# A decode attention kernel: one critical section with recorded semaphores, and a TensorE loop over six of the eight head groups

## The chip, the cores and the metric

The kernel runs on one core of one Trainium2 chip. The time is the device time of that core in microseconds (us), and the median of several runs is quoted. The span in the profile, from the first instruction to the last, is about 2 us shorter than the time.

## The reference

A decode step with adaptive layer norm: attention over a long cache, then a gated MLP mixer. The sizes are four sequences (B = 4), one new token each, 32 heads, 4096 cached positions, head size 128, width 512, all bf16. Cut to what matters:

```python
q = (h @ wq).reshape(B, Sq, H, Dh).transpose(0, 2, 1, 3)
scores = einsum('bhqd,bhkd->bhqk', q, k_cache) * Dh ** -0.5
p = softmax(scores)
o = einsum('bhqk,bhkd->bhqd', p, v_cache)
x = x + ga * (o.transpose(0, 2, 1, 3).reshape(B, Sq, H * Dh) @ wo)
h = layernorm(x) * (1 + cb) + sb
x = x + gb * gmlp(h, w_in, w_sp, b_sp, w_out)
```

The K and V caches are 268 MB of the 283 MB that the kernel reads.

## The kernel before

The work is cut into 32 quads: 8 groups of 4 heads, times 4 sequences. A quad loads 4 MiB of K and 4 MiB of V, each as 128 rows of 32 KB, one row per partition. VectorE multiplies K by q in two halves, TensorE sums over the head size with identity matmuls, VectorE folds and does the softmax, and TensorE multiplies by V one quad later.

```python
def load(cache, i, tag, parts):
    t = kvp.tile([P, NT * DH], BF16, name=tag, bufs=2)
    ...
        nc.sync.dma_start(out=t[:, a:b], in_=kv_view(cache, i)[:, a:b])
...
def scores(i, half):
    ...
    nc.vector.tensor_tensor(out=kt, in0=kt, in1=q[:, None, :].to_broadcast([P, HT, DH]), op=ALU.mult)
    ps = psum.tile([P, HT, DC], F32, name="s_ps", bufs=2)
    for cc in range(DH // DC):                       # 16 matmuls of 128x512
        nc.tensor.matmul(ps, lhsT=ident, rhs=kt[:, :, cc * DC:(cc + 1) * DC],
                         start=(cc == 0), stop=(cc == DH // DC - 1))
...
for i in range(NQ):                                  # 32 quads, written out
    if i + 1 < NQ:
        st["k", i + 1] = load_k(i + 1)
    if quads[i][1] == 0: ...                         # wo of this group, two buffers
    st["v", i] = load_v(i)
    if i == NQ - 1: ...                              # last wo, then w_in and w_out
    if i > 1:
        diagonal(i - 2)
    scores(i, 0)
    if i > 1:
        project(i - 2)
    scores(i, 1)
    fold(i, 0); fold(i, 1); softmax(i)               # order differs in the last quads
    if i > 0:
        values(i - 1)                                # 32 matmuls on V
    if i > 1:
        apply(i - 2)                                 # with wo, once per group
```

All tiles come from pools, a framework places the semaphores, and TensorE's whole instruction stream is straight-line.

## Time and profile before

| | before |
|---|---|
| time, median of three runs | 667.66 us (667.34 to 667.72) |
| span in the profile | 665.5 us |
| bytes read | 282.73 MB |
| rate in steady state | 432 GB/s, DMA share 1.00 |
| TensorE, VectorE busy | 62%, 61% |

The page of the kernel before. Its first line is the busy time of each engine (us, share of the span, instructions). The queue lines give packets, MB and the share of 16 DMA engines' span. Then comes the chain of work that ended last, by engine. Two lines of the costliest groups follow: the score matmuls and the fold, with busy time, mean ns of one, the engine's idle time before them and what ended it. The last line is the group of K loads: count, KB each, median us from issue to landing.

```profile
PE 415.7 (62%) x3024; PEld 204.6 (31%) x3024; DVE 402.6 (61%) x475; ACT 41.3 (6%) x115; POOL 4.7 (1%) x21
...
q1 hardware_dynamic: 12640, 282.73, 98.9%
q8 instruction: 23, 0.38, 0.2%
...
DMA 62%; PE 24%; DVE 12%; issue 0%; SPq 0%; ACT 0%; DVEq 0%
...
L281 PE MATMUL s_ps<-kt,ident 128*128 128x512 bf16 x1024 | 293.5, 457 | 185.5 <-DVE kt L276 185.5
...
L290 DVE TENSOR_REDUCE S<-s_ps 128x64 f32<-128x512 f32 x64 | 44.3, 692 | 125.5 <-PE s_ps L281 125.5
...
kt<-in_A_k_cache_dram SPq DMA_DIRECT2D x31, 4096.0 KB, 26.0
```

The hardware queue fills the engines (98.9% of their span). The second queue line counts the instruction fetches: 23 packets, 0.38 MB, so 16 KB each.

The stretches view of the same kernel: window, its length, then busy time and instruction count of PE, PEld, DVE, ACT and POOL, then the granted TensorE clock, the DMA share and GB/s.

```profile
60.00:300.00 240.00, 154.38 (x1036) 74.53 (x1035) 151.08 (x168) 12.59 (x39) 0.00 (x0) 0.77 1.00 432
300.00:600.00 300.00, 185.20 (x1209) 89.08 (x1209) 189.27 (x202) 14.46 (x45) 0.00 (x0) 0.76 1.00 432
```

In steady state the DMA engines do not rest (share 1.00).

The timeline of the sync engine, which issues nearly all loads (start us, us the issuing instruction took, engine, line, what):

```profile
0.75 0.37 SPq L74 DMA_DIRECT2D vt<-in_w_mod_dram  x1
...
643.21 0.37 SPq L444 DMA_DIRECT2D win_434<-in_B_w_in_dram  x1
648.07 1.44 SPq L444 DMA_DIRECT2D win_435<-in_B_w_in_dram  x1
650.51 0.34 SPq L446 DMA_DIRECT2D wout_436<-in_B_w_out_dram  x1
651.74 0.33 SPq L446 DMA_DIRECT2D wout_437<-in_B_w_out_dram  x1
663.16 0.36 SPq L545 DMA_DIRECT2D out_dram<-ot  x1
```

The first load is issued at 0.75 us, the output at 663.16 us, 2.3 us before the end of the span.

### The profile page before, as it was taken

To read this page: it belongs to the slowest core of one execution; us is meant where nothing else is said; L and a number is where in the kernel's file an instruction comes from. 1 tells how busy PE (TensorE), PEld (TensorE's weight loads), DVE (VectorE), ACT (ScalarE), POOL (GpSimd) and SP (SyncE) were. 2 spreads that over 40 slices of the span, in tenths; PEclk is the share of its full clock that TensorE was granted. 3 is DMA by queue.
4 is the path that set the end of the run, shared out by engine and by line. 5 is a ranking of instruction groups with operands and counts; after the bars stand their busy time and mean duration, and the time that the engine had idled before them with its cause. 6 is when DMAs were issued, how large, how long until landed. Compare 5 with 4: busy or idle time off the path is not lost.

```text
span 665.5 us, 6939 instructions
## 1 busy us (share of the span) xinstructions
PE 415.7 (62%) x3024; PEld 204.6 (31%) x3024; DVE 402.6 (61%) x475; ACT 41.3 (6%) x115; POOL 4.7 (1%) x21
## 2 busy tenths in 40 slices
PE   2557776655677655676555477654657655657775
PEld 2223333222333322233222233232223322223334
DVE  2166776675556576547666456666555666655762
ACT  1200000000000000000000000000000000000002
POOL 2000000000000000000000000000000000000000
PEclk9977777668887667887667788676888766888795
DMA  9999999999999999999999999999999999999995
GB/s 379 439 425 427 437 439 424 429 438 434 427 428 441 428 428 434 435 426 434 433 436 424 436 435 430 423 439 435 428 431 435 433 430 432 437 426 435 428 417 236
DMA packets 12749, 283.17 MB, mean 426 GB/s; under 512 B 1448, under 2 KB 1968, under 8 KB 4016
## 3 DMA queue, kind: packets, MB, share of 16 engines
q1 hardware_dynamic: 12640, 282.73, 98.9%
q8 instruction: 23, 0.38, 0.2%
q14 instruction: 6, 0.05, 0.0%
q0 software_dynamic: 64, 0.00, 0.0%
q10 hardware_dynamic: 16, 0.01, 0.0%
HBM read 282.73 MB, written 0.00 MB: 425 GB/s over the span
## 4 chain that ended last, share of the span: by engine, by line
DMA 62%; PE 24%; DVE 12%; issue 0%; SPq 0%; ACT 0%; DVEq 0%
DMA kt<-in_A_k_cache_dram 58%; PE s_ps L281 24%; DVE kt L276 11%; DMA vt<-in_A_v_cache_dram 3%; DMA wout_437<-in_B_w_out_dram 1%; PE big L341 0%; DVE S L290 0%; ACT E L311 0%; SPq L92 0%; DVE P_1_109 L314 0%; DVE P_0_105 L314 0%; PE y_ps L522 0%; DVE nm L308 0%; DVE mT L300 0%; SPq L78 0%
## 5 line engine op out<-in xcount | busy, mean ns | idle before, releaser
L281 PE MATMUL s_ps<-kt,ident 128*128 128x512 bf16 x1024 | 293.5, 457 | 185.5 <-DVE kt L276 185.5
L276 DVE TENSOR_TENSOR kt<-kt,qbc 128x8192 bf16<-128x8192 bf16 x64 | 282.7, 4420 | 82.9 <-DMA kt<-in_A_k_cache_dram 82.9
L281 PEld LDWEIGHTS <-ident 128*128 128x128 bf16 x1024 | 116.4, 114 | 351.1 <-issue 229.8
L290 DVE TENSOR_REDUCE S<-s_ps 128x64 f32<-128x512 f32 x64 | 44.3, 692 | 125.5 <-PE s_ps L281 125.5
L354 PE MATMUL zo_ps<-sel,osb 128*128 128x4 f32 x248 | 33.2, 257 | 26.6 <-ACT osb L347 26.6
L311 ACT ACTIVATE E<-S,nm 128x128 f32<-128x128 f32 x32 | 12.8, 401 | 563.4 <-DVE nm L308 563.4
L354 PEld LDWEIGHTS zo_ps<-sel,osb 128*128 128x128 f32 x248 | 30.6, 194 | 38.4 <-ACT osb L347 38.4
L341 PE MATMUL big<-vt,P_0_105 128*32 128x512 bf16 x352 | 21.0, 380 | 1.5 <-DMA vt<-in_A_v_cache_dram 1.5
L341 PE MATMUL big<-vt,P_1_109 128*32 128x512 bf16 x320 | 19.1, 380 | 0.0
L341 PE MATMUL big<-vt,P_2_113 128*32 128x512 bf16 x320 | 19.1, 380 | 0.0
L347 ACT COPY osb<-big 128x512 f32<-128x512 f32 x31 | 17.6, 566 | 20.0 <-PE big L341 20.0
L215 PE MATMUL big<-vt,hbc 128*32 128x512 bf16 x128 | 9.6, 471 | 5.2 <-DMA vt<-in_A_wq_dram 5.2
L314 DVE TENSOR_TENSOR P_1_109<-E,mask_99 128x512 bf16<-128x512 f32 x11 | 7.6, 692 | 6.8 <-ACT E L311 6.8
L314 DVE TENSOR_TENSOR P_0_105<-E,mask_99 128x512 bf16<-128x512 f32 x11 | 7.6, 692 | 6.7 <-ACT E L311 6.7
L341 PEld LDWEIGHTS <-P_0_105 128*32 128x32 bf16 x352 | 8.4, 96 | 8.9 <-DMA vt<-in_A_v_cache_dram 1.6
L314 DVE TENSOR_TENSOR P_2_113<-E,mask_99 128x512 bf16<-128x512 f32 x10 | 6.9, 692 | 6.2 <-ACT E L311 6.2
L400 PE MATMUL attn_ps<-oP,wo_g 128*128 128x4 bf16 x112 | 3.8, 164 | 10.6 <-DVE oP L397 10.6
L341 PEld LDWEIGHTS <-P_1_109 128*32 128x32 bf16 x320 | 7.6, 96 | 6.7
L341 PEld LDWEIGHTS <-P_2_113 128*32 128x32 bf16 x320 | 7.6, 96 | 6.7
L375 DVE TENSOR_TENSOR oT<-zo_ps,rz 128x4 bf16<-128x4 f32 x32 | 5.4, 168 | 7.1 <-PE zo_ps L363 6.0
L215 PEld LDWEIGHTS <-hbc 128*32 128x32 bf16 x128 | 4.4, 114 | 10.3 <-issue 8.4
L308 DVE STREAM_TRANSPOSE nm<-hb 128x32 f32<-128x32 f32 x32 | 6.8, 212 | 1.1
(221 smaller groups left out, 131.1 us busy)
## 6 DMA issues: line engine op xcount, KB each, us to landing
kt<-in_A_k_cache_dram SPq DMA_DIRECT2D x31, 4096.0 KB, 26.0
vt<-in_A_v_cache_dram SPq DMA_DIRECT2D x31, 4096.0 KB, 33.7
vt<-in_A_wq_dram SPq DMA_DIRECT2D x1, 4096.0 KB, 20.4
kt<-in_A_k_cache_dram SPq DMA_DIRECT2D x2, 2048.0 KB, 24.8
wo_g<-in_A_wo_dram SPq DMA_DIRECT2D x7, 512.0 KB, 26.5
vt<-in_w_mod_dram SPq DMA_DIRECT2D x1, 3072.0 KB, 9.8
vt<-in_A_v_cache_dram SPq DMA_DIRECT2D x1, 2048.0 KB, 17.8
win_434<-in_B_w_in_dram SPq DMA_DIRECT2D x1, 1344.0 KB
```

The lines of the kernel that those rows point to most:

```text
L215: nc.tensor.matmul(qp[hl * R:(hl + 1) * R, 0:n], lhsT=hbc[:, j, b, :], rhs=wv[:, g0:g0 + n, hl, :], start=(j == 0), stop=(j == J - 1), til ...
L276: nc.vector.tensor_tensor(out=kt, in0=kt, in1=q[:, None, :].to_broadcast([P, HT, DH]), op=ALU.mult,)
L281: nc.tensor.matmul(ps, lhsT=ident, rhs=kt[:, :, cc * DC:(cc + 1) * DC], start=(cc == 0), stop=(cc == DH // DC - 1),)
L290: nc.vector.tensor_reduce(out=st["S", i][:, half * HT:(half + 1) * HT], in_=st.pop(("s", i, half)), axis=AX.X, op=ALU.add,)
L308: nc.vector.transpose(out=nm, in_=hb)
L311: nc.scalar.activation(out=E, in_=S, func=AF.Exp, bias=nm[:, 0:1], scale=att_scale, accum_out=rs,)
L314: nc.vector.tensor_tensor(out=P4[:, 0:NT, :], in0=E[:, :, None].to_broadcast([P, NT, NH]), in1=mask4[:, None, :].to_broadcast([P, NT, NH]) ...
L341: nc.tensor.matmul(po[32 * t:32 * t + 32], lhsT=P4[:, n0:n0 + 8, :], rhs=st["v", i][:, n0:n0 + 4, :], start=(u == 0), stop=(u == NU - 1), ...
L347: nc.scalar.copy(out=osb, in_=po)
L354: nc.tensor.matmul(st["o", i], lhsT=osb[:, n, :], rhs=sel[:, NH * n:NH * n + NH], start=(n == 0), stop=(n == 3),)
L375: nc.vector.tensor_tensor(out=oT[:, :, b], in0=st.pop(("o", i)), in1=rz, op=ALU.mult,)
L400: nc.tensor.matmul(attn_ps[:, jo, :], lhsT=(wo_g[:, hl] if g < G - 1 else wo_l[hl // 2][:, hl % 2])[:, jo * P:(jo + 1) * P], rhs=oT[:, hl, :],
```

## The change

The intent is to take scheduling, buffers and semaphores out of the framework's hands, and to make TensorE's program short. A recorder collects every operation, works out which earlier ones it must wait for, and emits everything in one critical section, with one semaphore for each engine and one for each DMA buffer ("lane"). TensorE's instructions of groups 1 to 6 become one loop body of four quads, run six times, with waits that grow with the pass number. Fixed buffers replace the rotating ones, wo has one buffer and is loaded one group later, there are four P buffers instead of three, and w_in and w_out get lanes of their own. The diff, cut to its core:

```diff
+class Recorder:
+    ...                      # record(): what each operation must wait for
+    def emit(self, periods):
+        ...
+                if e == "tensor" and lo <= k < hi:
+                    if k == lo:
+                        with engine.Fori(0, periods, 1) as it:
+                            for group in body:
+                                ...
+                                    engine.wait_ge(sm, it * d + v)
+                                issue(group[0])
+                    continue
+                for w in o.waits:
+                    engine.wait_ge(sem(w), w.value)
+                issue(o)
...
-    nc = tc.nc
-    ctx.enter_context(tc.manual_schedule())
+    nc = Recorder(tc.nc, tc)
...
-        t = kvp.tile([P, NT * DH], BF16, name=tag, bufs=2)
+    kts = [kvp.tile([P, NT * DH], BF16, name=f"kt{a}", align_bytes=128) for a in range(2)]
+    vts = [kvp.tile([P, NT * DH], BF16, name=f"vt{a}", align_bytes=128) for a in range(2)]
...
-    NB = 3
+    NB = 4
...
-                    st["wo", g] = wk.tile([P, NH, D], BF16, name="wo_g", bufs=2)
-                    nc.sync.dma_start(out=st["wo", g], in_=wo_w[g])
+            if b == 0 and first > 0:
+                nc.sync.dma_start(out=wo_g, in_=wo_w[g - 1], lane="wo")
...
-                    nc.sync.dma_start(out=win[a], in_=win_v[:, j0:j1, :])
+                    nc.sync.dma_start(out=win[a], in_=win_v[:, j0:j1, :], lane=f"win{a}")
...
+        load(A_k_cache, kts[0], 0, 0, (1,), "k0")
+        for i in range(B + 1):
+            step(i // B, i % B, i)
+        nc.mark()
+        for i in range(B + 1, NQ - B + 1):
+            step(i // B, i % B)
+        nc.mark()
...
+        with tc.tile_critical():
+            nc.emit(G - 2)
```

## The prediction

> **What bounds the kernel now.** The DMA stream. The queue table gives the hardware queue 282.73 MB and 98.9% of the 16 engines' span. The windows view, in 40 us stretches from 60 to 620 us, shows a DMA share of 1.00 and 431 to 433 GB/s in every one. [...] The bytes take 282.73 / 0.432 = 654 us of the 665.5 us span; the rest is start and tail.

> The chain of waits names K loads 58%, score matmuls 24%, the VectorE multiply 11%. Compute is not critical: a K load takes 26 us from issue to landing, but its own 4.19 MB need only 9.7 us. So some 16 us of work is queued ahead of each, and K buffers could come free many us later before the engines idle. TensorE and VectorE each work about 25 of 40 us (two quads): 7 us of slack per quad.

> **What the change does.**
> - Same matmuls, VectorE and ScalarE work and bytes. K and V keep two buffers; the wo loads move one group later (0.5 MB, 1.2 us of stream) but stay before the last V load: 0.
> - The loop adds five backward branches. [...] No trace here shows how long; even 5 us falls where TensorE idles 5 to 7 us anyway (timeline before the first score matmul of a quad), with 16 us of queued DMA behind: 0. Instruction fetch is 0.2% of DMA; [...].
> - One semaphore per buffer instead of eight shared: w_in and w_out are issued with the last V load instead of at 643 to 652 us (the sync queue's waits: 13.7 and 1.9 us on earlier transfers). The stream ends near 658 instead of 661 us. But the tail follows the last V piece (653.0) and wo piece (654.3), which land as before; the matmuls on w_in wait for h (657.7), those on the second w_out half wait about 0.2 us: -0.2.
> - Weight loads are no longer issued ahead of their matmul's wait: about 0.1 us (one weight load's duration) on some three handovers of the tail: +0.3.
> - Entry and exit of the critical section: [...].
> - Start: group 0's wo no longer pads the queue before K load 3 (issued at 45.1 us, the queue lasting to about 48): +0.1.

> Sum: +0.5 us, all critical.

> **Prediction.** 668.2 us, 8 in 10 between 665.8 and 670.5. Faster by over 2%: 1%; within 2%: 97%; slower by over 2%: 2%.

> **What would show it.** Right: DMA share 1.00 at 432 GB/s in every 40 us window, span within 2 us of 665.5; w_in and w_out issued near 631 us; TensorE idle at loop edges without a dip of DMA. Wrong on the loop: DMA share below 0.95 in slices 80 us apart. Wrong on the tail: clearly other than 12 us from the last V landing to the end.

> **What would make it wrong.** Instruction fetch taking over 15 us per loop edge; other SBUF addresses of K and V changing the DMA rate; early w_in loads overtaking the last V pieces.

The terms that are left come to +0.2 us (0, 0, −0.2, +0.3, +0.1). The sum of +0.5 us also holds the +0.3 us of the cut term, an estimate for which no measured number was named. The loop's 0: TensorE waits 185.5 us in 33 waits for VectorE's product on the page before, 5.6 us each in the mean.

## More of the kernel before

The two compute engines have idle time, but that alone does not say how much compute could be added: the engines take turns (on the page TensorE waits 185.5 us for VectorE's product, and VectorE 125.5 us for TensorE's sums). The chain of work that ended last, in order of time (start us, us, what), shows it at the start, where data for the first quads is already there:

```profile
31.29 4.43 DVE kt L276
35.77 9.28 PE s_ps L281 x32
45.07 0.70 DVE S L290
...
48.48 4.34 DVE kt L276
52.85 9.27 PE s_ps L281 x32
...
69.93 9.27 PE s_ps L281 x32
```

From one quad's score matmuls to the next is 17.08 us (52.85 − 35.77, and again 69.93 − 52.85). This is the serial compute cycle: multiply 4.4, matmuls 9.3, fold 0.7, softmax and a remainder of 2.7. Further on a quad takes about 19.7 us of stream, an estimate from its 8.52 MB (K, V and a quarter of wo) at the 432 GB/s above, so only some 2.6 us per quad are to spare.

## The result, and the profile after

| | before | after |
|---|---|---|
| time, median of four runs | 667.65 us (667.34 to 667.72) | 668.40 us (668.39 to 668.53) |
| ratio after to before | | 1.0012 (95%: 0.9995 to 1.003) |
| span of the profiled run | 665.5 us | 666.6 us |
| granted TensorE clock, mean | 0.771 | 0.775 |
| instruction fetches | 23 | 11 |

A ratio here is the mean time of one kernel's fast runs over that of the other's in the same rounds, so it is not quite the ratio of the medians quoted. Every run of the changed kernel is slower than every run of the one before, by about 0.75 us. The profiled run of the kernel before took 667.26 us, 0.4 us below its median; the two profiles therefore differ by 1.1 us instead of 0.75.

The page of the changed kernel, same lines as before:

```profile
PE 412.8 (62%) x3025; PEld 200.0 (30%) x3025; DVE 403.0 (60%) x475; ACT 41.2 (6%) x115; POOL 5.8 (1%) x23
...
q1 hardware_dynamic: 12640, 282.73, 98.8%
q8 instruction: 11, 0.18, 0.1%
...
DMA 62%; PE 24%; DVE 12%; ACT 1%; issue 1%; SPq 0%; DVEq 0%
```

Bytes, packets and engine work are the same, but there are 12 instruction fetches fewer. The stretches view of the changed kernel, columns as above:

```profile
60.00:300.00 240.00, 150.63 (x1033) 72.47 (x1031) 152.79 (x168) 12.53 (x39) 0.00 (x0) 0.77 1.00 431
300.00:600.00 300.00, 187.43 (x1212) 88.21 (x1213) 189.21 (x202) 14.45 (x45) 0.00 (x0) 0.76 1.00 432
```

The stream still binds. The timeline of the sync engine in the changed kernel:

```profile
0.97 0.37 SPq L142 DMA_DIRECT2D vt_71<-in_w_mod_dram  x1
...
632.79 0.47 SPq L142 DMA_DIRECT2D win_146<-in_B_w_in_dram  x1
633.31 16.73 SPq L142 DMA_DIRECT2D win_147<-in_B_w_in_dram  x1
650.08 0.47 SPq L142 DMA_DIRECT2D wout_148<-in_B_w_out_dram  x1
650.59 0.43 SPq L142 DMA_DIRECT2D wout_149<-in_B_w_out_dram  x1
663.78 0.36 SPq L142 DMA_DIRECT2D out_dram<-ot  x1
```

Three things are to be read here. The first load is issued 0.22 us later. From output issue to end of span there are 2.8 us instead of 2.3 (666.6 − 663.78 against 665.5 − 663.16, rounded; the exact ends give +0.52). And w_in is issued 10 us earlier, but its second issuing instruction stays for 16.73 us, so w_out goes out at 650 us, nearly as before. What held that instruction the trace doesn't show.

The view by source line of the loop's own instructions in the changed kernel (operation, count, ns minimum/median/maximum, first and last start):

```profile
L153 PEldq COMPARE_BRANCH  x6: 83/218/233, 192.1 to 587.5; - x6
```

The timeline of TensorE around the first loop edge, which this branch makes at 192.1 us:

```profile
191.72 1.91 PE L142 MATMUL bank_87<-vt_72,P_3_99 128*32 128x512 bf16 x32
194.71 1.05 PE L142 MATMUL bank_91<-sel,osb_140 128*128 128x4 f32 x8 [1.07 <-ACT osb_140 L142]
```

The first matmul after the edge waits for ScalarE's copy, as in every quad, and starts 0.05 us after it. The edge shows a branch of 0.2 us (218 ns in the median of six) and no other cost. Among the 16 KB instruction packets in the trace (queue q8), one starts at 192.0 us and the next at 615.0 us, so none starts in the five repeats (the branches lie between 192.1 and 587.5 us). Queue q14 has six instruction packets of 8 KB in either kernel, with and without the loop. So the repeats start none of the 16 KB fetches; this does not yet say whether the loop gains time.

The last view is not one of the page's. It sums the durations of single DMA packets in each trace. There are 8064 packets of 32 KB, most of them rows of K and V; "DMA work" is the sum of the durations of all packets that start within the span, over 16 engines.

| kernel | 32 KB packets of exactly 1213 ns | mean, ns | fetches | DMA work, us |
|---|---|---|---|---|
| before | 99.6% | 1214.53 | 23 | 659.35 |
| after | 68.2% | 1215.47 | 11 | 659.46 |

In the changed kernel nearly a third of the packets take 1 to 13 ns longer, which no other view shows: the share stays 1.00, and GB/s moves in its last digit. Still the DMA work is the same within 0.11 us. Something made the packets slower and something else gave that time back. The experiments take the two apart.

### The profile page after: what moved, and what is told of

The parts are those of the page before. It is cut to its first block, busy times and chain, and to the rows that moved or that the text cites. A ratio compares the mean times of both kernels' runs of the same rounds, so it can differ in the third digit from the quotient of the medians.

```text
span 666.6 us, 6933 instructions
## 1 busy us (share of the span) xinstructions
PE 412.8 (62%) x3025; PEld 200.0 (30%) x3025; DVE 403.0 (60%) x475; ACT 41.2 (6%) x115; POOL 5.8 (1%) x23
## 3 DMA queue, kind: packets, MB, share of 16 engines
q1 hardware_dynamic: 12640, 282.73, 98.8%
HBM read 282.73 MB, written 0.00 MB: 424 GB/s over the span
## 4 chain that ended last, share of the span: by engine, by line
DMA 62%; PE 24%; DVE 12%; ACT 1%; issue 1%; SPq 0%; DVEq 0%
DMA kt_69<-in_A_k_cache_dram 58%; PE bank_88 L142 14%; DVE kt_69 L142 11%; PE bank_89 L142 9%; DMA wo_l_145<-in_A_wo_dram 3%; DVE kt_70 L142 1%; SPq L142 0%; PE bank_87 L142 0%; ACT L142 0%; PE bank_84 L142 0%; DVE S_117 L142 0%; DVE S_118 L142 0%; DVE P_1_95 L142 0%; DVE P_0_93 L142 0%; DVE x1b L142 0%
## 5 line engine op out<-in xcount | busy, mean ns | idle before, releaser
L142 DVE TENSOR_TENSOR kt_69<-kt_69,qbc 128x8192 bf16<-128x8192 bf16 x32 | 141.4, 4420 | 53.8 <-DMA kt_69<-in_A_k_cache_dram 53.8
L142 DVE TENSOR_TENSOR kt_70<-kt_70,qbc 128x8192 bf16<-128x8192 bf16 x32 | 141.4, 4420 | 33.5 <-DMA kt_70<-in_A_k_cache_dram 33.4
L142 PE MATMUL bank_88<-kt_70,ident 128*128 128x512 bf16 x256 | 91.1, 535 | 94.4 <-DVE kt_70 L142 94.4
L142 PE MATMUL bank_88<-kt_69,ident 128*128 128x512 bf16 x256 | 90.0, 529 | 96.0 <-DVE kt_69 L142 96.0
L142 PEld LDWEIGHTS bank_88<-kt_70,ident 128*128 128x128 bf16 x256 | 31.9, 130 | 148.0 <-DVE kt_70 L142 96.6
L142 PEld LDWEIGHTS bank_88<-kt_69,ident 128*128 128x128 bf16 x256 | 31.6, 129 | 147.9 <-DVE kt_69 L142 97.3
L142 PE MATMUL bank_89<-kt_70,ident 128*128 128x512 bf16 x256 | 57.9, 379 | 0.0
L142 PE MATMUL bank_89<-kt_69,ident 128*128 128x512 bf16 x256 | 57.9, 379 | 0.0
L142 PEld LDWEIGHTS bank_89<-kt_69,ident 128*128 128x128 bf16 x256 | 25.0, 98 | 30.2 <-DVE kt_69 L142 0.2
L142 PEld LDWEIGHTS bank_89<-kt_70,ident 128*128 128x128 bf16 x256 | 25.0, 98 | 30.3 <-DVE kt_70 L142 0.3
L142 PE MATMUL bank_91<-sel,osb_140 128*128 128x4 f32 x120 | 15.8, 255 | 15.7 <-ACT osb_140 L142 15.7
L142 PE MATMUL bank_90<-sel,osb_139 128*128 128x4 f32 x128 | 16.7, 254 | 9.3 <-ACT osb_139 L142 9.3
L142 PEld LDWEIGHTS bank_91<-sel,osb_140 128*128 128x128 f32 x120 | 14.5, 191 | 23.1 <-ACT osb_140 L142 23.1
L142 PEld LDWEIGHTS bank_90<-sel,osb_139 128*128 128x128 f32 x128 | 15.5, 191 | 13.7 <-ACT osb_139 L142 13.7
L142 DVE TENSOR_REDUCE S_118<-bank_89 128x64 f32<-128x512 f32 x8 | 5.5, 692 | 22.1 <-PE bank_89 L142 22.1
L142 DVE TENSOR_REDUCE S_117<-bank_89 128x64 f32<-128x512 f32 x8 | 5.5, 692 | 22.1 <-PE bank_89 L142 22.1
L142 DVE TENSOR_REDUCE S_119<-bank_89 128x64 f32<-128x512 f32 x8 | 5.5, 692 | 22.1 <-PE bank_89 L142 22.1
L142 DVE TENSOR_REDUCE S_120<-bank_89 128x64 f32<-128x512 f32 x8 | 5.5, 692 | 19.9 <-PE bank_89 L142 19.9
L142 PE MATMUL bank_86<-vt_71,P_2_97 128*32 128x512 bf16 x256 | 15.3, 380 | 1.5 <-DMA vt_71<-in_A_v_cache_dram 1.5
L142 PE MATMUL bank_86<-vt_71,P_0_93 128*32 128x512 bf16 x256 | 15.3, 380 | 0.0
L142 PE MATMUL bank_87<-vt_72,P_1_95 128*32 128x512 bf16 x256 | 15.3, 380 | 0.0
L142 PE MATMUL bank_87<-vt_72,P_3_99 128*32 128x512 bf16 x224 | 13.4, 380 | 0.0
```

The lines of the kernel that those rows point to most:

```text
L142: i = getattr(getattr(self.nc, o.eng), o.method)(*o.args, **o.kw)
```

## The experiments

Every edited version of the changed kernel has the loop written out, as in the first experiment, and is to be compared with that one. The column "excess" is the median less that of the kernel before in the same rounds; the groups ran on different chips, so excesses are compared across groups.

| run | rounds | median, us | before, us | excess, us | ratio (95%) | mean 32 KB packet, ns | DMA work, us |
|---|---|---|---|---|---|---|---|
| after (loop) | | 668.40 | 667.65 | 0.75 | 1.0012 (0.9995–1.003) | 1215.47 | 659.46 |
| u_unrolled | 5 | 669.57 | 667.55 | 2.02 | 1.003 (1.0018–1.0043) | 1215.98 | 660.65 |
| b_crit_end | 5 | 668.63 | 667.55 | 1.08 | 1.0016 (1.0003–1.0028) | 1214.54 | 659.47 |
| u_late | 5 | 669.49 | 667.55 | 1.94 | 1.0028 (1.0016–1.0041) | 1215.99 | 660.61 |
| u_addr | 5 | 669.63 | 667.55 | 2.08 | 1.0031 (1.0017–1.0045) | 1215.95 | 660.59 |
| u_al256 | 5 | 668.18 | 667.55 | 0.63 | 1.0009 (0.9997–1.0022) | 1214.53 | 659.52 |
| b_off128 | 5 | 670.66 | 667.55 | 3.11 | 1.0046 (1.0032–1.006) | 1218.45 | 662.22 |
| u_al_wo | 5 | 667.99 | 667.41 | 0.58 | 1.0009 (0.9995–1.0022) | 1214.59 | 659.32 |
| u_fetch | 5 | 669.44 | 667.41 | 2.03 | 1.0032 (1.0018–1.0046) | 1215.01 | 659.93 |
| u_busy4 | 3 | 671.01 | 667.41 | 3.60 | 1.0056 (1.004–1.0071) | 1217.27 | 661.22 |
| u_busy8 | 3 | 701.79 | 667.55 | 34.24 | 1.0513 (1.0496–1.053) | | |
| u_lessv | 3 | 612.90 | 667.55 | −54.65 | 0.9181 (0.9168–0.9194) | | |

The ratios' intervals are about ±0.13%, or 0.9 us. The medians are far tighter: runs of one kernel lie within 0.4 us of each other except in u_busy8 (3). Differences under 0.2 us are not read as anything.

### u_unrolled: the same section, semaphores and buffers, without the loop

```diff
-                if e == "tensor" and lo <= k < hi:
+                if e == "tensor" and lo <= k < hi and False:
```

> The changed kernel with its TensorE loop written out (same recorder, same critical section, same order; only the loop is gone). Theory (the stream bounds it; the loop is free): within 0.5 us of the changed kernel, at 668.4 to 668.9 us, a little slower if anything because instruction fetch goes back from 0.18 MB to about 0.38 MB (0.2 MB / 0.432 = 0.46 us of stream). Rival (the loop's edges and register waits cost time): 0.5 us or more faster than the changed kernel, 667.9 us or less.

It took 669.57 us, 1.2 us more than with the loop (excess 2.02 against 0.75). The theory that the loop neither costs nor gains missed by its size, and the rival, that the loop costs, has the wrong sign. The loop gains. The page of this kernel:

```profile
q8 instruction: 23, 0.38, 0.2%
```

Written out, the 12 instruction fetches are back, and the DMA work rises from 659.46 to 660.65 us: 1.19 us, the size of the whole difference. The fetches themselves take 1.51 us of 16 engines here and 0.71 us with the loop, 0.80 us less. There are also about as many 32 KB packets of some 1.7 us instead of 1.2 us as there are fetches (25 here, 14 with the loop), which adds 11 × 0.5 / 16, or 0.34 us. So a fetch of 16 KB costs a full stream about 0.1 us, and 12 cost 1.1 to 1.2 (20 of the 25 long packets, and 9 of the 14 with the loop, overlap a fetch in time).

It also follows that the rest of the change costs 2.0 us. The next runs look for it.

### b_crit_end: an empty critical section at the end of the kernel before

```diff
         tile_adaLN_cond__mha_block_cached__mixer_gmlp__decode_kernel(tc, *args)
+        with tc.tile_critical():
+            sem = tc.alloc_semaphore("s_none")
+            for e in (nc.sync, nc.scalar, nc.gpsimd, nc.vector, nc.tensor):
+                e.wait_ge(sem, 0)
```

> The kernel before, followed by a critical section that every engine enters, waits there for a semaphore that is already satisfied, and leaves. It measures what one entry and exit cost at the end. In the changed kernel's trace the time from the issue of the output transfer to the end of the span is 2.82 us against 2.34 us before. Theory: +0.5 us (0.3 to 0.8) over the kernel before, all of it after the output transfer. Rival (the exit is hidden behind the landing of the output, the extra 0.5 us comes from elsewhere): within 0.15 us of before.

It took 1.08 us more. The timeline of the sync engine in this kernel, whose span is 666.7 us:

```profile
663.28 0.36 SPq L545 DMA_DIRECT2D out_dram<-ot  x1
```

The output is issued as before (663.28 against 663.16), and 3.4 us instead of 2.3 pass from there to the end: nearly all of the cost comes after the output. This section pays its entry and its exit after the work. In the changed kernel the entry lies at the start (first load +0.22 us) and the exit at the end (+0.52 us), together 0.74 us. A critical section costs about 0.7 to 1.1 us here, more than twice the estimate of 0.3 us.

### u_late: w_in and w_out issued late again

```diff
-... in_=win_v[:, j0:j1, :], lane=f"win{a}")
+... in_=win_v[:, j0:j1, :], lane=("v1", "v1_1")[a])
-... in_=wout_v[a], lane=f"wout{a}")
+... in_=wout_v[a], lane=("v1_2", "v1_3")[a])
```

> The unrolled kernel, but the w_in and w_out transfers wait for pieces of the last V load again (issued at about 643 to 652 us as in the kernel before). In the changed kernel the last V piece is used at 653.85 us against 653.03 before. Theory A (early w_in transfers share the engines with the last V pieces and delay them): the last V piece 0.3 to 0.8 us earlier than in the unrolled kernel, and the time 0.2 to 0.6 us shorter. Theory B (the 0.8 us come from the start and the packet rate): same as the unrolled kernel within 0.2 us.

The loads shared lanes with V pieces, so they were issued between 649.73 and 654.17 us. The time was 669.49 us, the same as u_unrolled. When w_in and w_out are issued is worth nothing in this range: they are not what the tail waits for.

### u_addr: V buffers placed ahead of K buffers

```diff
-    kts = [kvp.tile(..., name=f"kt{a}", align_bytes=128) for a in range(2)]
     vts = [kvp.tile(..., name=f"vt{a}", align_bytes=128) for a in range(2)]
+    kts = [kvp.tile(..., name=f"kt{a}", align_bytes=128) for a in range(2)]
```

> The unrolled kernel with the two V buffers below the two K buffers in SBUF, as they lie in the kernel before. The mean duration of a 32 KB packet was 1215.5 ns in the changed kernel and 1214.5 ns before, worth 8064 x 1.0 ns / 16 = 0.5 us. Theory A (the addresses set the packet time): mean back at 1214.5 ns and 0.4 to 0.6 us shorter than the unrolled kernel. Theory B (that difference is drift from run to run): same as the unrolled kernel within 0.2 us.

669.63 us, and a mean packet of 1215.95 ns: nothing changed. But the order of the buffers is not the only thing about their addresses. The start addresses in SBUF, in bytes per partition, were then compared:

| kernel | buffers start at | off a multiple of 256 |
|---|---|---|
| before | 56064, 88832, 121600, 154368 | none |
| after, u_unrolled, u_addr | 57728, 90496, 123392, 156288 | all but the third, by 128 |
| u_al256 | 58368, 91136, 124160, 157184 | none |
| b_off128 | 56192, 88960, 121728, 154496 | all, by 128 |

The kernel before has all four buffers at multiples of 256 bytes without having asked for it. The changed kernel asks for 128 and gets three that are off. Exchanging K and V left three off. The mean 32 KB packet takes 1214.53 ns in the kernel before and 1215.47 to 1215.98 ns in the three with three buffers off. Whether the start address is what lengthens a packet was put to the test from both sides.

### u_al256: all loaded buffers at multiples of 256

```diff
-    kts = [kvp.tile([P, NT * DH], BF16, name=f"kt{a}", align_bytes=128) for a in range(2)]
-    vts = [kvp.tile([P, NT * DH], BF16, name=f"vt{a}", align_bytes=128) for a in range(2)]
+    kts = [kvp.tile([P, NT * DH], BF16, name=f"kt{a}", align_bytes=256) for a in range(2)]
+    vts = [kvp.tile([P, NT * DH], BF16, name=f"vt{a}", align_bytes=256) for a in range(2)]
 ...     # the same for wo_g, wo_l, win and wout
```

> The unrolled kernel with the K, V and weight buffers placed at multiples of 256 bytes in SBUF instead of 128 (before they all lie at 256 modulo 512; in the changed kernel three of the four K and V buffers start 128 bytes off a multiple of 256). In the kernel before over 99% of the 32 KB packets take exactly 1213 ns; in the changed and the unrolled kernels about 30% take 1214 to 1225 ns. Theory A (a start off the 256-byte boundary lengthens a packet): all packets back at 1213 ns, mean about 1214.5 ns, and the time 0.5 to 1.0 us below the unrolled kernel's 669.57 us. Theory B (the longer packets come from something else in the recorder's program, such as the times of issue or the semaphores): packets and time as in the unrolled kernel within 0.2 us.

The time fell to 668.18 us, an excess of 0.63 instead of 2.02: 1.39 us less than u_unrolled. 99.5% of the packets take 1213 ns again, and the DMA work falls by 1.13 us. What is left, 0.63 us, fits entry and exit (0.74) less a slightly shorter tail; no run takes these two apart.

### b_off128: the kernel before, with all four buffers off by 128

```diff
+    pad = persist.tile([P, 64], BF16, name="pad")
+    nc.gpsimd.memset(pad, 0.0)
     rows = persist.tile([2 * B, D], BF16, name="rows")
```

> The kernel before with one unused 128-byte tile ahead of the others, so that every K, V and weight buffer starts 128 bytes off a multiple of 256. Theory A (alignment): a good part of the 32 KB packets longer than 1213 ns, mean 1215.5 ns or more, and 0.5 to 2 us slower than before. Theory B (something else in the recorder's program): packets at 1213 ns and the time of before within 0.2 us.

128 bytes of padding ahead of everything made the kernel before 3.1 us slower. 75% of its packets take longer than 1213 ns, the mean is 3.9 ns longer (1218.45 against 1214.53), and the DMA work rises by 2.87 us. The stretches view of this kernel, columns as above:

```profile
60.00:300.00 240.00, 155.31 (x1040) 74.62 (x1037) 150.41 (x168) 12.56 (x39) 0.00 (x0) 0.77 1.00 430
300.00:600.00 300.00, 184.86 (x1206) 88.68 (x1207) 187.34 (x199) 14.45 (x45) 0.00 (x0) 0.76 1.00 431
```

The DMA share is 1.00 as ever, while the rate falls from 432 to 430 and 431 GB/s. Engines that are busy all the time move bytes less well here. With this, alignment is shown in both directions. With three of four buffers off, only some 30% of the packets lengthen, and with four, 75%. The order of the packets in the traces says which loads are spared. Counted in order of start, 128 of the 32 KB packets to a load and from the ninth load on, a load into an unaligned buffer has 64% of its packets lengthened in the changed kernel when the load before it in the queue (wo, which is aligned, included) was unaligned too (27 loads), and 9% when it was aligned (14 loads); loads into the aligned buffer have 0 to 15%, and as loads overlap, some of that belongs to their neighbours. u_addr, where other loads are the ones behind an aligned one, gives 68% and 11%. In b_off128 every load comes behind an unaligned one: 79% (only its first three loads, 1 to 10%, are nearly spared). Why this is so stays open.

### u_al_wo: aligned, and wo loaded early into two buffers as before

```diff
-        wo_g = wk.tile([P, NH, D], BF16, name="wo_g", align_bytes=128)
+        wo_gs = [wk.tile([P, NH, D], BF16, name=f"wo_g{a}", align_bytes=256) for a in range(2)]
...
-            if b == 0 and first > 0:
-                nc.sync.dma_start(out=wo_g, in_=wo_w[g - 1], lane="wo")
+            if b == 0 and g < G - 1:
+                nc.sync.dma_start(out=wo_gs[g % 2], in_=wo_w[g], lane=f"wo{g % 2}")
```

> The aligned unrolled kernel with two wo buffers, each group's wo loaded at the start of that group, as in the kernel before. Theory (the order of the wo loads is free because the stream has no gap either way): same as u_al256 within 0.2 us. Rival (the wo loads moved back cost part of what is left between u_al256, 668.18 us, and before, 667.55 us): 0.2 to 0.5 us faster than u_al256.

667.99 us, an excess of 0.58 against 0.63 for u_al256. The later wo with its single buffer is free, as predicted.

### u_fetch: more instructions, so more fetches

```diff
+            for _ in range(32):      # in values(), after zsum, on top of u_al256
+                nc.tensor.matmul(po[:, 0, 0:4], lhsT=ident, rhs=wide[:, 0:4], start=True, stop=True)
```

> The aligned unrolled kernel (u_al256) with 32 extra matmuls of 4 columns ahead of the value matmuls of each quad (31 quads), where TensorE would idle: 992 matmuls and their weight loads, 127 KB of instructions or 8 more fetches of 16 KB. In the profiles 12 fetches fewer (the loop against the unrolled kernel) went with 1.04 us less DMA work and 1.15 us less time. Theory (each fetch of 16 KB costs about 0.09 us of a saturated stream): 0.5 to 0.9 us slower than u_al256 and 8 more instruction packets. Rival (fetches are free; the loop was faster for another reason): within 0.2 us of u_al256.

The page of this kernel:

```profile
q8 instruction: 31, 0.51, 0.3%
```

There are 8 fetches more (31 against 23; 0.51 MB against 0.38, near the 127 KB expected), and the time is 1.45 us above that of u_al_wo on the same chip (669.44 against 667.99), where fetches at 0.1 us each would give 0.8. The direction agrees and the size does not. The DMA work rose by only 0.61 us over u_al_wo (659.93 against 659.32). The added matmuls lengthen TensorE's turn by under 1 us per quad (from 60 to 600 us PE is busy for 359.08 us against 340.82 in u_al_wo, or 0.7 us for each of some 27 quads), which by the next two runs should be hidden, and the packets show no gap. The last matmul on V ran 1.0 us later than in u_al_wo (654.7 against 653.7), so most of the loss lies in the stream. Why it is larger than the sum of the durations says is open. This run can't separate the fetches from the matmuls that bring them: for each fetch it gives 0.08 us by DMA work and 0.18 us by time, against 0.1 us from the loop. The gain of the loop rests on its own comparison, not on this one.

### u_busy4 and u_busy8: how much compute the stream hides

```diff
+                if cc == DH // DC - 1:
+                    for _ in range(8):       # 4 in u_busy4; per half quad, adds zero
+                        nc.tensor.matmul(s_pss[half], lhsT=ident, rhs=wide, start=False, stop=False)
```

> The unrolled kernel with 8 more matmuls of 512 columns per half quad on TensorE (they add zeros to the scores), so 16 per quad or about 4.5 us at 0.28 us each. Theory (the stream bounds it and TensorE has 7 us to spare per quad): at most 0.7 us slower than the unrolled kernel. Rival (the chain of waits read literally: score matmuls 24% of the span): every second quad's extra time is added, 16 x 4.5 = 72 us or more.

The 16 extra matmuls of a quad take 3.8 us (8 take 1.89 us in the trace; the 4.5 us expected were an estimate, close to the page before, where 1024 score matmuls take 293.5 us, 0.29 us each). By the 7 us of slack in the prediction they should have vanished; with no slack at all they would have cost 3.8 × 32, or 122 us. They cost 32.2 us over u_unrolled (34.24 − 2.02), or 1.0 us per quad. Both expectations missed, and the slack is what lies between: 3.8 − 1.0, or about 2.8 us per quad. The timeline of u_busy8 shows a cycle that has become compute (the bracket is the idle time before and what ended it):

```profile
296.47 4.42 DVE L142 TENSOR_TENSOR kt<-kt,qbc 128x8192 bf16<-128x8192 bf16 x1
300.94 5.60 PE L142 MATMUL bank<-kt,ident 128*128 128x512 bf16 x15 [3.67 <-DVE kt L142]
...
313.70 0.69 DVE L142 TENSOR_REDUCE S<-bank 128x64 f32<-128x512 f32 x1 [4.49 <-PE bank L142]
...
316.20 0.69 DVE L142 TENSOR_TENSOR P<-E,mask 128x512 bf16<-128x512 f32 x1 [0.56 <-ACT E L142]
...
317.02 4.42 DVE L142 TENSOR_TENSOR kt<-kt,qbc 128x8192 bf16<-128x8192 bf16 x1
```

Multiply, matmuls, fold, softmax, next multiply: 20.55 us (317.02 − 296.47), each step waiting for the one before. TensorE waits for VectorE (3.67) and VectorE waits for TensorE (4.49) in the same quad, so their idle time can't be filled by adding work to one of them. And K is no longer what the multiply waits for: it starts right behind the softmax.

> The unrolled kernel with 4 more matmuls per half quad (8 per quad, about 1.9 us). The run with 16 per quad showed a serial cycle of 20.5 us per quad: first VectorE multiply 4.4, score matmuls 12.7, fold 0.7, softmax 2.6, then the next multiply. Without extra matmuls that cycle is about 17 us, against 19.5 us of stream per quad. Theory (slack is the difference, 2.5 us or so, not 7): 8 extra matmuls make it about 19 us, still hidden: at most 1 us slower than the unrolled kernel. Rival (no slack at all, each extra us counts): 32 x 1.9 = 60 us slower, or half of that.

Half of that, 1.9 us per quad, costs 1.58 us in all over u_unrolled (3.60 − 2.02), so 0.05 us per quad: hidden. Of the 1.58, a gap of 0.4 to 0.5 us in the DMA lies at 48 to 51 us, about when the work queued at the start runs out, and 0.57 us is more DMA work (two more fetches and somewhat longer packets). The rest is not attributed. The expectation of at most 1 us was missed by that. Between them the two runs put the slack between 1.9 and 3.8 us, and the cycle of 17.1 us read from the trace before, against 19.7 us of stream, says 2.6.

### u_lessv: a quarter of V not loaded in groups 1 to 6

```diff
-            load(..., (2, 4, 8, 16, 16) if last else (1,), f"v{b % 2}")
+            load(..., (2, 4, 8, 16, 16) if last else (2, 4) if 1 <= g <= 6 else (1,), f"v{b % 2}")
```

> Wrong on purpose: in groups 1 to 6 only three quarters of each V load are fetched (the rest is what an earlier load left). 24 x 1.05 MB = 25.2 MB less. Theory (the stream bounds it): 25.2 / 0.432 = 58 us faster than the unrolled kernel, about 611 us. Rival (the chain through K loads, VectorE and TensorE bounds it): little faster, above 650 us.

This kernel computes something wrong on purpose (its output still passed the comparison, so the comparison does not test V closely). The page of this kernel:

```profile
HBM read 257.56 MB, written 0.00 MB: 421 GB/s over the span
```

It reads 25.2 MB less and takes 56.7 us less than u_unrolled (excess −54.65 against 2.02), where 25.2 MB at 432 GB/s are 58.3 us. The time follows the bytes: the stream binds, and the compute cycle is hidden, even though a quad now takes only about 17.3 us of stream (an estimate, 7.47 MB at 432 GB/s), just above the 17.1 us cycle.

### loop_sizes: two small loops of tiny matmuls after the end of u_al256, beside 44 more cache loads

```diff
+        for body, turns in ((300, 4), (1200, 4)):
+            with self.nc.tensor.Fori(0, turns, 1):
+                for _ in range(body):
+                    self.nc.tensor.matmul(*self.idle[0], **self.idle[1])
```

> The aligned unrolled kernel; after its output two TensorE loops of 4 passes are added, of 300 and of 1200 small matmuls with their weight loads (38 KB and 154 KB of instructions), beside 44 more cache loads that keep the DMA engines busy. The time means nothing. In the changed kernel 11 fetches of 16 KB served a program whose loop body of 41 KB ran six times, so the body was fetched once. Theory (TensorE keeps more than 41 KB of instructions and goes back within that for nothing): no fetch and no gap at the edges of the small loop; the large loop fetches again on every pass, with a gap at each edge. Rival (going back never fetches): 4 x 154 KB cost only 10 fetches and no gap.

The sizes of 38, 154 and 41 KB in it are estimates, at 128 bytes of instructions for a matmul with its weight load: 300, 1200 and, for a pass of the changed kernel's loop, 328 of them (41 KB of 1024 bytes). The trace below agrees with that figure, with 128 matmuls to a stretch and a fetch of 16 KB.

This was one look, of unknown state; its time (1105 us) means nothing, and only its trace is used. The timeline of TensorE in this run:

```profile
673.06 31.00 PE L174 MATMUL bank<-wide,ident 128*128 128x4 bf16 x1154 [2.90 <-issue]
...
743.42 3.56 PE L174 MATMUL bank<-wide,ident 128*128 128x4 bf16 x128 [2.64 <-issue]
749.34 2.46 PE L174 MATMUL bank<-wide,ident 128*128 128x4 bf16 x87 [2.37 <-issue]
757.98 2.54 PE L174 MATMUL bank<-wide,ident 128*128 128x4 bf16 x89 [6.18 <-issue]
```

And the view by source line of the loops' branches:

```profile
L172 PEldq COMPARE_BRANCH  x8: 76/226/6572, 673.7 to 946.1; - x8
```

### What was not run

The version to try next is the changed kernel with its loop and with buffers at multiples of 256. From the runs, 668.40 − 1.39, it should take about 667.0 us, an estimate, and so perhaps 0.6 us less than the kernel before. It was not run. No version that was run beats the kernel before.

## Why the prediction was right or wrong

The total was right (668.2 predicted, 668.40 measured), and so was its main reason: the stream of K and V binds, the change leaves the bytes as they are, so nothing large can happen. u_lessv shows that directly. But the sum was right because two misses of opposite sign cancel; that it came within 0.2 us is luck.

The ledger, in excess over the kernel before:

| step | predicted, us | measured, us | shown by |
|---|---|---|---|
| loop | 0 | −1.2 to −1.3 | u_unrolled against after |
| K, V and weight buffers off by 128 | 0 (named as a risk) | +1.4 | u_al256, b_off128 |
| entry and exit of the section | +0.3 (estimate) | +0.74 | both traces; b_crit_end |
| tail: earlier w_in and w_out, weight loads | +0.1 | −0.2 | both traces; u_late |
| start | +0.1 | 0 | sums of packets |
| wo one group later | 0 | 0 | u_al_wo |
| sum | +0.5 | +0.7 (measured: 0.75) | |

Point by point:

- **"What bounds the kernel now: the DMA stream."** Right. The share is 1.00 at 431 to 432 GB/s in the changed kernel too.
- **"7 us of slack per quad."** Wrong: about 2.7 us. The step that failed is reading slack off an engine's idle time. Both engines idle because each waits for the other within a quad. The slack is the stream's time per quad less the serial cycle, 19.7 − 17.1, and u_busy4 and u_busy8 bracket it. The 16 us of work queued ahead of a K load, which the prediction took as a reserve too, did not help: a turn longer than the stream's comes again in every quad, as in u_busy8 (20.55 against 19.7 us, and 32 us in all), where the K loads landed 14.6 us after their issue instead of 26.0.
- **The loop: 0.** This is the step that failed most. That every pass fetches its body anew, so that nothing is saved, was an assumption that no trace showed. The runs show otherwise: after the first pass, or a packet early in the second, bodies of 39 KB (after: no 16 KB fetch starts between 192.0 and 615.0 us) and of 38 KB (loop_sizes: none between 676.6 and 703.4 us) are not fetched again, and one of 154 KB is (42 packets in its four passes). The loop saves 12 fetches, and in this saturated stream they are worth 1.2 us.
- **"Other SBUF addresses of K and V changing the DMA rate"** was listed as what would make the prediction wrong, without a number. It happened, at +1.4 us. The start addresses of both kernels could have been read in advance.
- **Entry and exit.** Right in kind, mis-sized: 0.22 + 0.52 us, against the +0.3 us. The prediction named no number that its estimate came from.
- **"Weight loads: about 0.1 us on some three handovers."** Too large. One weight load takes 0.1 us (96 to 114 ns in the mean for bf16 on the page before), and in a quad looked at, the first one of the score matmuls did start 4.46 us ahead of its matmul before (259.08 against 263.54 us) and does not after (261.96 against 261.97). But from the end of h to the first matmul on w_in it takes 0.15 us before (657.66 to 657.81) and 0.15 after (658.49 to 658.64), the same within a few hundredths.
- **"w_in and w_out are issued with the last V load"; "issued near 631 us."** Half right: w_in at 632.79 and 633.31, w_out at 650.08 and 650.59, because the second issue took 16.73 us. **"The stream ends near 658 instead of 661 us"** was too much: between 659 and 660 us the DMA engines are still busy for 0.22 of the time, against 0.49 before, and the last packet of the loads ends at 661.2 us, against 660.6 before. u_late shows that this order is worth nothing. From the last use of V to the output issue it takes 9.72 us after and 9.92 before, a gain of 0.2 as predicted, but its reason is not shown.
- **"TensorE idle at loop edges without a dip of DMA."** Right: the branch takes 0.2 us, and TensorE waits for ScalarE there as everywhere.
- **"Start: +0.1."** Not seen: summed over packets, no microsecond from 3 to 640 us has idle DMA engines in either kernel.

What stays open: why an unaligned load behind an aligned one is nearly spared; what held the w_in issue for 16.7 us; and where part of the cost of u_fetch comes from.

## What to carry to other kernels

In this kernel, bound by a stream that is busy all the time, the remaining differences were in what the stream spends on each byte. So where the DMA share is 1.00, look at the durations of single packets, put loaded buffers at multiples of 256 bytes (1.39 us in u_al256), and count instruction fetches, which a loop can save (12 of them, 1.2 us, with a body of 39 KB here; the one of 154 KB in loop_sizes was fetched anew in its passes). Read slack as stream time less the serial compute cycle (2.6 us per quad here), never as an engine's idle time (7 us). And when a large rewrite moves the time little, take it apart before calling it neutral: here a gain of 1.2 us was hidden behind an alignment that costs 1.4.
